# Decayed block attention and a SiLU layer on one core: the order of the up units, two state casts and two loads around chunks 8 to 11

## The chip, the core and the metric

The kernel runs on one core of a Trainium2 chip. The metric is device time in microseconds (us) of one execution; lower is better. Five engines work from queues of their own, each strictly in order, and wait for each other by semaphores: TensorE (PE in the profile; PEld is its loading of weights), VectorE (DVE), ScalarE (ACT), GpSimd (POOL) and SyncE (SP), which here only issues DMA transfers. ScalarE can issue transfers too; they then stand in its own queue between its other instructions.

## The reference: what is computed

Inputs are q, k, v of shape (4, 8, 768, 64) (batch, head, position, width), a decay `lam` per head, and two weight matrices. Per batch entry and head, in blocks of 64 positions:

```python
intra = np.einsum('bhic,bhjc->bhij', qb, kb) * Dmask[None]       # lam ** (i - j) for i >= j
intra = np.einsum('bhij,bhjd->bhid', intra, vb)
inter = np.einsum('bhid,bhde->bhie', qb * lam_pow[None], kv_state)
out[:, :, sl] = intra + inter
kv_state = lam_block * kv_state + np.einsum('bhsd,bhse->bhde', kb * rev_pow, vb)
...
h = x @ w_in                       # x: (3072, 512), heads side by side; w_in: (512, 2048)
g = h * (1.0 / (1.0 + np.exp(-h)))
return g @ w_out                   # w_out: (2048, 512)
```

(`lam_block` is written with its axes in the full text.) The output is 3072 x 512 float32.

## The kernel before

**Chunks and groups.** The 3072 tokens are 24 chunks of 128 (two attention blocks of 64 each; six chunks are one batch entry) and 12 groups of 256, so group g is made of chunks 2g and 2g+1. A chunk's attention comes first; its transposed output (`xt`) is the input of the dense layer of its group. The kernel's own schedule is kept as written: each engine's queue holds its instructions in the order in which the code emits them. Chunks 0 to 3 and groups 0 and 1 follow a list written out by hand (`ORDER`, L23). Everything that the change touches comes later and is written as loops from L902 on.

**What a chunk from 6 on goes through.** `load_qk` and `load_vs` (L880, L892) issue its q, k and v, 256 KB each, by `load_1` (L229), on SP unless an engine is named. The buffers: 4 for q (`qf`), 6 for k (`kf`), 6 for v (`vf`). `preps` (L897) scales q and k by the decay on GpSimd (L364, L365: two instructions each for q and k, four a chunk). `transposes` issues two DMA transposes on SP (L390, L391), which leave `qt` and `kn`. `vcast` (L382) rounds v to bfloat16 (`vb`), on ScalarE unless another engine is named. Then `section` (L438) does the attention with small 64 x 64 matmuls (L540), for up to three jobs at once: outputs (`op`) of the chunks `outs`, scores (`sp`) of the chunks `scores`, and state increments (`kv_ps`) of the half chunks `states`. Outputs need the masked scores (`ss`), `vb`, `qt` and the running states as bfloat16 (`kvs`). Behind the matmuls the section emits the move of the outputs to `xt`, the masking of the scores on VectorE (L560), and, for each half chunk of `states`, an addition to the running total on VectorE (`total`, L571 or L573) and a cast of it to `kvs` (L574, helper `move` at L176) on the engine named by `cast`. With `defer=True` this last part, additions and casts, is not emitted but handed back as a function, `finish`.

**What a group goes through.** Eight up units (`ups`, L951): unit i is 8 matmuls (`ffn1_mm`, L605) into one bank of 512 columns (`h_ps`, two such banks) and one SiLU on ScalarE (L621); it makes features 256 i to 256 i + 255. Units 2j and 2j+1 fill one tile `quad(g, j)`. The down product (`seven`, L731) does 7 half-width products where 8 would be plain, so it needs sums and differences of the SiLU's results as well: `gd` of one quad (`g_diff`, L711), and `gc` and `gb` of the quads j-2 and j (`g_cross`, L698), on VectorE. `ups` emits `g_diff` behind the units 1, 3 and 5 and `g_cross` behind 5 and 7; the last `gd` comes in the second product's step (`after_4`). The order of the products is 3, 4, 1, 6, 5, 2, 7: the first two take the SiLU's results directly, product 1 needs `gc`, 6 and 7 need `gd`, 5 and 2 need `gb`.

**The order around the change.** The lines from L922 on, in order: the scalings and transposes of chunks 4 and 5; pieces of the down product of groups 0 and 1 (`down0`); casts of the last weights; q and k of chunk 8, issued by ScalarE (L934); the section with scores of 4 and 5 and three states, cast by ScalarE (L936); three more pieces of down product; the scalings and transposes of 6 and 7; the section with the outputs of 4 and 5 (L941); two pieces of down product with `load_qk(9)` on SP between them (L943); the second half of the weight sums (L946). Then the loop over the groups 2 to 10 (L959), in which c and d are the chunks of the next group and a and b those of the one after it. In group 2 the scores of 6 and 7 come ahead of the third product and the outputs of 6 and 7 ahead of the sixth. In group 3 the scores of 8 and 9 come ahead of the last up unit (L971, `defer=True`); ahead of the third product stand the v casts of 10 and 11, then `late()` with the additions and casts for 8 and 9, then the scalings and transposes of 12 and 13 and more loads; ahead of the sixth product comes the section with outputs of 8 and 9, scores of 10 and 11 and their states (L993, states cast by GpSimd). From group 4 on each group has one section, ahead of its sixth product.

Of the kernel before, what the change touches and what calls it, by code (L numbers as in the profile page):

```python
# [36 lines left out]
def kernel(  # L37
# [10 lines left out]
    nc = tc.nc  # L48
# [121 lines left out]
    def cast_w(which, i, e="D", part=None):  # L170
        a, b = (0, 2) if part is None else (part, part + 1)
        ko, f = w_piece(which, i, a, b)
        t = wtmp[which, i]
        move(e, (w_in_bf if which == "in" else w_out_bf)[:, ko, f], t[part] if isinstance(t, list) else t[:, a:b, :])

    def move(e, dst, src):  # L176
        if e == "A":
            nc.scalar.activation(dst, src, AF.Copy)  # L178
        elif e == "P":
            nc.gpsimd.tensor_copy(dst, src)  # L180
        else:
            nc.vector.tensor_copy(dst, src)  # L182
# [46 lines left out]
    def load_1(src, c, tag, bufs, e=None):  # L229
        b, blk = divmod(c, NB)  # L230
        t = io.tile([128, H, D], F32, name=tag, tag=tag, bufs=bufs)
        (e or nc.sync).dma_start(out=t, in_=src[b, :, blk * BLK:(blk + 1) * BLK, :].rearrange("h s d -> s h d"))
        return t

    def load_k(c, e=None):
        rawk[c] = load_1(k, c, "kf", 6, e)
# [145 lines left out]
    def vcast(c, e="A"):  # L382
        if c in vraw:
            move(e, natb[c][2], vraw.pop(c).rearrange("s (p j) d -> s p j d", j=2))
# [40 lines left out]
    def new_xt(c):  # L425
        g, off = group_of[c]
        if off == 0:
            xt[g] = xpool.tile([128, KO_IN, GROUPS[g]], BF16, name="xt", tag="xt", padded_shape=[128, KO_IN, 512])
        return xt[g][:, :, off * BLK:(off + 1) * BLK]
# [8 lines left out]
    def section(outs=(), scores=(), states=(), e="AA", tags=(("att", 3),) * 2, spare=None, cast="D", defer=False):  # L438
# [33 lines left out]
        def place(c, h):  # L472
            w = [x for x, y in states if y == h].index(c)
            return kv[0][:, h] if shared else kv[h][:, w]
# [70 lines left out]
        for c in outs:  # L545
            x = new_xt(c)
        if outs:
            if len(outs) == 2:
                x = xt[group_of[outs[0]][0]]
            for i, op in enumerate(banks):  # L550
                if len(tags) == 4:
                    i, w = divmod(i, 2)
# [3 lines left out]
        if scores:  # L556
# [5 lines left out]
                both.append(ss)  # L562
            for w, c in enumerate(scores):
                st[c] = [ss[:, NP * w:NP * w + NP, :] for ss in both]
        def finish():
            for c, h in states:
                b = c // NB
                kvs = nat.tile([128, NP, D], BF16, name="kvs", tag="kvs", bufs=8)
                old, total[b] = total.get(b), nat.tile([128, NP, D], F32, name="total", tag="total", bufs=4)
                if old is None:  # L570
                    nc.vector.tensor_copy(total[b], place(c, h))  # L571
                else:
                    nc.vector.tensor_tensor(total[b], old, place(c, h), op=AL.add)  # L573
                move(cast, kvs, total[b])  # L574
                kvh[(c, 1) if h == 0 else (c + 1, 0)] = kvs

        if defer:
            return finish
        finish()

    kvh = {}
    mask64 = const.tile([128, 64], F32, name="mask64")
# [13 lines left out]
    total = {}  # L596
# [28 lines left out]
    def ffn1_two(g, i):  # L625
        tick()
        ffn1_open(g, i)
        ffn1_mm(g, i, range(KO_IN))
        ffn1_close(g, i)
# [68 lines left out]
    def g_cross(g, j):  # L698

        low, one = quad(g, j - 2), quad(g, j)  # L700
        cross = sum_tile(g, "gc", 0, 128)[:, j - 2]
        nc.vector.tensor_tensor(cross, low[:, :, lo], one[:, :, hi], op=AL.add)  # L702
        both = gpool.tile([128, 4, 256], BF16, name="gb", tag="g")
        nc.vector.tensor_tensor(both, low, one, op=AL.add)  # L704
        for u in range(4):
            k = 4 * (j - 2) + u
            gs[g, 1, k] = cross[:, u, :]
            gs[g, 5, k] = both[:, u, lo]
            gs[g, 2, k] = both[:, u, hi]

    def g_diff(g, j):  # L711

        one = quad(g, j)
        d = sum_tile(g, "gd", j // 2, 128)[:, j % 2]
        a, b = (hi, lo) if j < 2 else (lo, hi)
        nc.vector.tensor_tensor(d, one[:, :, a], one[:, :, b], op=AL.subtract)  # L716
        for u in range(4):
            gs[g, 6 if j < 2 else 7, 4 * (j % 2) + u] = d[:, u, :]
# [100 lines left out]
    for word in LOADS.split():  # L819
        a = int(word[2])  # L820
# [59 lines left out]
    def load_qk(*cs, e=None):  # L880
        for c in cs:
            if c < NCHUNK:
                rawq[c] = load_1(q, c, "qf", 4, e)
                load_k(c, e)
                loaded.append(c)

    def transposes(*cs):
        for c in cs:
            if c < NCHUNK:
                dma_t(c)  # L890

    def load_vs(*cs, e=None):  # L892
        for c in cs:
            if c < NCHUNK:
                load_v(c, e)

    def preps(*cs):  # L897
        for c in cs:
            if c < NCHUNK:
                prep(c)  # L900
# [16 lines left out]
    def down0(kk, *mts):  # L917
        for mt in mts:
            ffn2(mt // 2, mt % 2, range(4 * kk, 4 * kk + 4), tag="h" if mt > 1 else "o")
# [11 lines left out]
    copy_kt(5, tk5)  # L931
    vcast(4), vcast(5)
    cast_w("out", 6), cast_w("out", 7, "A", 0), cast_w("out", 7, "A", 1)
    load_qk(8, e=nc.scalar)  # L934
    down0(2, 0)
    section((), (4, 5), ((4, 0), (4, 1), (5, 0)), cast="A")  # L936
    down0(2, 1)
    down0(3, 2)
    down0(3, 3)
    preps(6, 7), transposes(6, 7)  # L940
    section((4, 5), (), (), "AD", (("att", 3), ("kv", 1), ("att", 3), ("att", 3)))  # L941
    down0(3, 0)
    load_qk(9)  # L943
    down0(3, 1)
    for i in range(len(WSUMS)):
        weight_sum(i, 1)  # L946
# [1 line left out]
    def steps(*cs):  # L948
        return [(c, h) for c, h in [(cs[0] - 1, 1)] + [(c, h) for c in cs for h in range(2)] if c > 5][:-1]

    def ups(g, i):  # L951
        ffn1_two(g, i)
        if i > 3 and i % 2:
            g_cross(g, i // 2)
        if i % 2 and i < 7:
            g_diff(g, i // 2)

    many = (("h", 2),) * 2 + (("att", 3),) * 2
    for g in range(2, len(GROUPS) - 1):  # L959
        c, d, a, b = range(2 * g + 2, 2 * g + 6)  # L960
        for i in range(8):
            if g == 2 and i == 4:
                preps(8, 9)
                load_qk(10)
                transposes(8, 9)
                load_vs(8, 9)
                load_qk(11)
            if g < 4 and i in (4, 5):
                vcast(c + i % 2)
            if g == 3 and i == 7:  # L970
                late = section((), (c, d), steps(c, d), cast="A", defer=True)  # L971
            ups(g, i)
        for i, unit in enumerate(seven(g)):
            if i == 2 and g > 2:
                vcast(a)
                if g == 3:
                    vcast(b)
                    late()
            if i == 2:
                preps(c + 4, d + 4)  # L980
                transposes(c + 4, d + 4)
                load_qk(*([12] if g == 2 else []), c + 7)
                load_vs(c + 6, d + 6)
                load_qk(d + 7)
            if i == 2 and g == 2:
                section((), (c, d), steps(c, d), cast="A")
            if i == 3 and g > 3:
                vcast(b)
            if i == 0 and g == 2:
                load_vs(10, 11)  # L990
            if i == 5:
                cs = [x for x in (a, b) if g > 2 and x < NCHUNK]
                section((c, d), cs, steps(*cs) if cs else (), "AD", many[:2] if cs else many, cast="P")  # L993
            unit()
    g = len(GROUPS) - 1
    for i in range(8):
        ups(g, i)
# [32 lines left out]
```

## Time and profile before

| what | us |
|---|---|
| median of 3 runs | 202.52 (200.32 to 202.88) |
| the profiled execution, its own time | 200.34 |
| its span, first to last instruction | 198.0 |
| TensorE busy with matmuls in the span | 188.5 |
| VectorE, ScalarE, GpSimd busy | 131.2, 102.3, 71.3 |
| group 2, from its first up matmul to that of group 3 | 47.90 to 63.49 |
| group 3 | 63.49 to 80.03 |
| group 4 | 80.03 to 94.94 |
| group 5 | 94.94 to 109.34 |

How to read it: the span is what the profile sees; 2.34 us of the execution's own time lie around it. The rows on groups are read off the chain of work that ended last, in order of time. A timeline line gives the start, the time taken, engine, line, operation, the names written and read, and the count; brackets give how long the engine stood idle before it and who ended that. ACTq and SPq are the queues of ScalarE and SP, with the issues of DMA transfers in them. Granted TensorE clock: 1.00 throughout.

### The profile page before, as it was taken

To read this page: it belongs to the slowest core of one execution; us is meant where nothing else is said; L and a number is where in the kernel's file an instruction comes from. 1 tells how busy PE (TensorE), PEld (TensorE's weight loads), DVE (VectorE), ACT (ScalarE), POOL (GpSimd) and SP (SyncE) were. 2 spreads that over 40 slices of the span, in tenths; PEclk is the share of its full clock that TensorE was granted. 3 is DMA by queue.
4 is the path that set the end of the run, shared out by engine and by line. 5 is a ranking of instruction groups with operands and counts; after the bars stand their busy time and mean duration, and the time that the engine had idled before them with its cause. 6 is when DMAs were issued, how large, how long until landed. Compare 5 with 4: busy or idle time off the path is not lost.

```text
span 198.0 us, 6663 instructions
## 1 busy us (share of the span) xinstructions
PE 188.5 (95%) x2844; PEld 151.1 (76%) x2844; DVE 131.2 (66%) x254; ACT 102.3 (52%) x192; POOL 71.3 (36%) x124
## 2 busy tenths in 40 slices
PE   7688999999999999999999999999999999999993
PEld 2457544546887887887888888888888887888882
DVE  1896459778986296985875855865785666565263
ACT  3874875153825855553554563563662752633621
POOL 5240000918826060793653724742760201200000
PEclk9999999999999999999999999999999999999999
DMA  3999999989679995995988949998999790200203
GB/s 105 338 370 404 403 408 304 243 235 271 115 171 129 208 192 131 204 203 125 213 121 202 196 111 227 144 207 221 126 310 368 111 358 22 106 0 3 109 0 106
DMA packets 95581, 38.71 MB, mean 196 GB/s; under 512 B 80960, under 2 KB 88640, under 8 KB 95552
## 3 DMA queue, kind: packets, MB, share of 16 engines
q1 hardware_dynamic: 93328, 37.76, 75.8%
q10 hardware_dynamic: 2224, 0.53, 1.2%
q8 instruction: 22, 0.36, 0.7%
q14 instruction: 7, 0.06, 0.1%
HBM read 27.27 MB, written 6.29 MB: 170 GB/s over the span
## 4 chain that ended last, share of the span: by engine, by line
PE 76%; DVE 7%; DMA 5%; POOL 3%; SPq 3%; ACT 3%; issue 2%; ACTq 0%; DVEq 0%; POOLq 0%
PE h_ps L609 32%; PE o_ps L729 23%; PE o_ps L654 6%; PE h_ps L843 5%; PE op L540 3%; SPq L224 2%; DMA pair<-in_q_dram 2%; PE o_last L729 2%; DVE ss L560 2%; PE sp L540 1%; DVE total L573 1%; DMA qf<-in_q_dram 1%; DMA kn<-kb 1%; ACT g L621 1%; POOL kvs L180 1%
## 5 line engine op out<-in xcount | busy, mean ns | idle before, releaser
L609 PE MATMUL h_ps<-xt,w_in_bf 128*128 128x256 bf16 x672 | 75.9, 273 | 0.0
L609 PEld LDWEIGHTS <-w_in_bf 128*128 128x128 bf16 x672 | 65.5, 98 | 8.5 <-issue 0.2
L621 ACT ACTIVATE g<-h_ps 128x512 bf16<-128x512 f32 x84 | 49.9, 597 | 33.5 <-PE h_ps L609 33.5
L364 POOL TENSOR_TENSOR qb<-qf,lam_fwd 128x256 bf16<-128x256 f32 x18 | 12.0, 667 | 40.5 <-issue 25.4
L716 DVE TENSOR_TENSOR gd<-g 128x512 bf16<-128x512 bf16 x40 | 20.5, 515 | 8.2 <-ACT g L621 8.0
L180 POOL CAST kvs<-total 128x256 bf16<-128x256 f32 x26 | 11.0, 433 | 25.6 <-DVE total L573 20.0
L178 ACT ACTIVATE xt<-op 128x256 bf16<-128x256 f32 (+1 forms) x18 | 8.3, 486 | 21.9 <-PE op L540 20.9
L729 PE MATMUL o_ps<-w_out_bf,gb 128*128 128x256 bf16 x144 | 18.9, 273 | 0.5 <-issue 0.5
L182 DVE CAST xt<-op 128x256 bf16<-128x256 f32 (+1 forms) x16 | 8.3, 543 | 16.1 <-PE op L540 14.4
L729 PE MATMUL o_ps<-wsum,gd 128*128 128x256 bf16 x144 | 18.7, 273 | 0.0
L702 DVE TENSOR_TENSOR gc<-g 128x512 bf16<-128x512 bf16 x20 | 9.7, 484 | 13.2 <-ACT g L621 13.2
L729 PE MATMUL o_ps<-wsum,g 128*128 128x256 bf16 x144 | 17.2, 273 | 0.0
L729 PEld LDWEIGHTS <-g 128*128 128x128 bf16 x160 | 15.7, 98 | 1.8
L729 PEld LDWEIGHTS <-gd 128*128 128x128 bf16 x160 | 15.6, 98 | 1.8
L729 PEld LDWEIGHTS <-gb 128*128 128x128 bf16 x160 | 14.9, 98 | 2.6 <-issue 0.6
L364 POOL TENSOR_TENSOR kb<-kf,lam_bwd 128x256 bf16<-128x256 f32 x20 | 14.6, 731 | 3.9 <-DMA kf<-in_k_dram 2.9
L704 DVE TENSOR_TENSOR gb<-g 128x1024 bf16<-128x1024 bf16 x20 | 15.9, 798 | 0.0
L573 DVE TENSOR_TENSOR total<-total,kv_ps 128x256 f32<-128x256 f32 x33 | 13.8, 419 | 2.2
L654 PE MATMUL o_ps<-w_out_bf,g 128*128 128x512 bf16 x64 | 15.0, 379 | 0.1
L365 POOL TENSOR_TENSOR kb<-kf,lam_bwd 128x256 bf16<-128x256 f32 x20 | 14.4, 718 | 0.0
L365 POOL TENSOR_TENSOR qb<-qf,lam_fwd 128x256 bf16<-128x256 f32 x18 | 13.0, 721 | 0.0
L560 DVE TENSOR_TENSOR ss<-sp,mask 128x512 bf16<-128x512 f32 x20 | 12.8, 681 | 0.0
(105 smaller groups left out, 247.0 us busy)
## 6 DMA issues: line engine op xcount, KB each, us to landing
vf<-in_v_dram SPq DMA_DIRECT2D x20, 256.0 KB, 4.4
kf<-in_k_dram SPq DMA_DIRECT2D x19, 256.0 KB, 4.7
qf<-in_q_dram SPq DMA_DIRECT2D x17, 256.0 KB, 4.2
pair<-in_moe_w_out_dram SPq DMA_DIRECT2D x8, 512.0 KB, 7.7
pair<-in_moe_w_in_dram SPq DMA_DIRECT2D x6, 512.0 KB, 7.5
out_dram<-pair SPq DMA_DIRECT2D x12, 256.0 KB, 3.8
out_dram<-ob SPq DMA_DIRECT2D x10, 256.0 KB, 3.8
pair<-in_k_dram SPq DMA_DIRECT2D x4, 256.0 KB, 4.5
```

Of the source, the lines that this page charges most:

```text
L180: nc.gpsimd.tensor_copy(dst, src)
L364: eng.tensor_tensor(dst[:, 0::2], src[:, 0::2, ::-1, :], by[:, 0::2, ::-1, :], op=AL.mult)
L365: eng.tensor_tensor(dst[:, 1::2], src[:, 1::2], by[:, 1::2], op=AL.mult)
L560: nc.vector.tensor_tensor(ss, sp.rearrange("k w p q -> k (w p) q"), mask64[:, None, :].to_broadcast([128, len(scores) * NP, D]), op=AL.mult)
L573: nc.vector.tensor_tensor(total[b], old, place(c, h), op=AL.add)
L609: nc.tensor.matmul(hps[g, i][:, a:a + 256], lhsT=w_in_bf[:, ko, m * 128:(m + 1) * 128], rhs=xt[g][:, ko, :], start=(ko == 0 and u == 0), s ...
L621: nc.scalar.activation(gg.rearrange("p u n -> p (u n)"), hps[g, i], AF.Silu)
L654: nc.tensor.matmul(o, lhsT=gt[g, ko][:, mt * BLK:(mt + 1) * BLK], rhs=w_out_bf[:, ko, :], start=(ko == 0), stop=(ko == KO_OUT - 1))
L704: nc.vector.tensor_tensor(both, low, one, op=AL.add)
L716: nc.vector.tensor_tensor(d, one[:, :, a], one[:, :, b], op=AL.subtract)
L729: nc.tensor.matmul(dst, lhsT=lhsT, rhs=rhs, start=(start and k == 0), stop=(k == K2 - 1), skip_group_check=True)
L843: nc.tensor.matmul(hps["m", m], lhsT=w_in_bf[:, ko, m * 128:(m + 1) * 128], rhs=xall[0][:, :, ko, :], start=(ko == 0), stop=(ko == KO_IN - 1))
```

## The change

Five edits, one text:

- q and k of chunk 9 are issued by ScalarE directly behind those of chunk 8; the issue on SP at L943 goes.
- `ups` takes a position n and does the units in the order 0, 1, 4, 5, 2, 3, 6, 7, in all groups from 2 on. What follows a unit (`g_diff`, `g_cross`) goes with it.
- In group 3 the section with scores and states of chunks 8 and 9 is emitted ahead of the seventh position in place of the eighth.
- A deferred section now hands back a function that emits the additions alone and gives the list of casts. In group 3 the additions are emitted behind the unit of the seventh position, and the four casts, still on ScalarE, ahead of the third product.
- The v casts of 10 and 11 in group 3 go from ScalarE to GpSimd, where they stand ahead of the scalings of 12 and 13.

```diff
--- before.py
+++ after.py
@@ -562,7 +562,8 @@
                 both.append(ss)
             for w, c in enumerate(scores):
                 st[c] = [ss[:, NP * w:NP * w + NP, :] for ss in both]
-        def finish():
+        def sums():
+            casts = []
             for c, h in states:
                 b = c // NB
                 kvs = nat.tile([128, NP, D], BF16, name="kvs", tag="kvs", bufs=8)
@@ -571,12 +572,15 @@
                     nc.vector.tensor_copy(total[b], place(c, h))
                 else:
                     nc.vector.tensor_tensor(total[b], old, place(c, h), op=AL.add)
-                move(cast, kvs, total[b])
+                casts.append((kvs, total[b]))
+                if not defer:
+                    move(cast, *casts[-1])
                 kvh[(c, 1) if h == 0 else (c + 1, 0)] = kvs
+            return casts
 
         if defer:
-            return finish
-        finish()
+            return sums
+        sums()
 
     kvh = {}
     mask64 = const.tile([128, 64], F32, name="mask64")
@@ -931,7 +935,7 @@
     copy_kt(5, tk5)
     vcast(4), vcast(5)
     cast_w("out", 6), cast_w("out", 7, "A", 0), cast_w("out", 7, "A", 1)
-    load_qk(8, e=nc.scalar)
+    load_qk(8, 9, e=nc.scalar)
     down0(2, 0)
     section((), (4, 5), ((4, 0), (4, 1), (5, 0)), cast="A")
     down0(2, 1)
@@ -940,7 +944,6 @@
     preps(6, 7), transposes(6, 7)
     section((4, 5), (), (), "AD", (("att", 3), ("kv", 1), ("att", 3), ("att", 3)))
     down0(3, 0)
-    load_qk(9)
     down0(3, 1)
     for i in range(len(WSUMS)):
         weight_sum(i, 1)
@@ -948,7 +951,9 @@
     def steps(*cs):
         return [(c, h) for c, h in [(cs[0] - 1, 1)] + [(c, h) for c in cs for h in range(2)] if c > 5][:-1]
 
-    def ups(g, i):
+    def ups(g, n):
+
+        i = (0, 1, 4, 5, 2, 3, 6, 7)[n]
         ffn1_two(g, i)
         if i > 3 and i % 2:
             g_cross(g, i // 2)
@@ -967,16 +972,20 @@
                 load_qk(11)
             if g < 4 and i in (4, 5):
                 vcast(c + i % 2)
-            if g == 3 and i == 7:
-                late = section((), (c, d), steps(c, d), cast="A", defer=True)
+            if g == 3 and i == 6:
+                sums = section((), (c, d), steps(c, d), defer=True)
             ups(g, i)
+            if g == 3 and i == 6:
+                late = sums()
         for i, unit in enumerate(seven(g)):
-            if i == 2 and g > 2:
+            if i == 2 and g > 3:
                 vcast(a)
+            if i == 2 and g == 3:
+                for x in late:
+                    move("A", *x)
+            if i == 2:
                 if g == 3:
-                    vcast(b)
-                    late()
-            if i == 2:
+                    vcast(a, "P"), vcast(b, "P")
                 preps(c + 4, d + 4)
                 transposes(c + 4, d + 4)
                 load_qk(*([12] if g == 2 else []), c + 7)
```

## The prediction

> **What bounds the kernel now.** I read the page first, then the busy time by window, then TensorE's timeline wherever a window shows less than a full PE, then what those gaps waited for.
>
> ```profile
> PE 188.5 (95%) x2844; PEld 151.1 (76%) x2844; DVE 131.2 (66%) x254; ACT 102.3 (52%) x192; POOL 71.3 (36%) x124
> ...
> q10 hardware_dynamic: 2224, 0.53, 1.2%
> ```
>
> TensorE is the bound: 188.5 of 198.0 us. The first 20 us and the last 4 hold most of the 9.5 us without a matmul, and the change touches neither. From 20 us on, only a stall of PE is worth time. The second line is ScalarE's DMA queue: today it carries two loads of 256 KB (q and k of chunk 8) and little else. The change gives it four.
>
> ```profile
> 75.80:78.10 2.30, 1.90 (x129) 1.54 (x128) 0.92 (x3) 0.99 (x3) 0.00 (x0) 1.00 0.39 89
> 91.30:93.00 1.70, 1.33 (x121) 1.17 (x120) 0.00 (x0) 0.00 (x0) 0.00 (x0) 1.00 0.44 99
> 106.30:107.50 1.20, 1.20 (x122) 1.16 (x122) 0.00 (x0) 0.00 (x0) 0.30 (x1) 1.00 1.21 272
> ```
>
> Each window is one attention section (outputs of two chunks, scores and states of the next two) inside a group. The columns are the window, its length, then busy time and count of PE, PEld, DVE, ACT, POOL. The section of some 128 small matmuls takes 1.2 us when nothing is late (106.3; the next ones, read off the chain, take 1.23, 1.21, 1.13). It takes 2.3 at 75.8 and 1.7 at 91.3: 1.1 and 0.5 us lost.
>
> ```profile
> 61.03 0.22 PE L540 MATMUL op<-qt,kvs 64*64 64x64 bf16 x4 [0.23 <-ACT kvs L178]
> ...
> 76.47 0.22 PE L540 MATMUL op<-qt,kvs 64*64 64x64 bf16 x2 [0.17 <-ACT kvs L178]
> ...
> 76.92 0.22 PE L540 MATMUL op<-qt,kvs 64*64 64x64 bf16 x2 [0.23 <-ACT kvs L178]
> ...
> 92.27 0.32 PE L540 MATMUL sp<-qt,kn 64*64 64x64 bf16 x16 [0.37 <-DMA kn<-kb]
> ```
>
> The brackets say who was late: at 61.0 and 76.5 a state cast on ScalarE, at 92.3 a transposed k. VectorE's and SP's timelines say why:
>
> ```profile
> 73.98 0.41 DVE L763 TENSOR_TENSOR msum<-msum,o_ps 128x256 f32<-128x256 f32 x1
> 74.31 0.41 DVE L716 TENSOR_TENSOR gd<-g 128x512 bf16<-128x512 bf16 x1
> 74.64 1.77 DVE L573 TENSOR_TENSOR total<-total,kv_ps 128x256 f32<-128x256 f32 x4
> ```
>
> The four totals of chunks 8 and 9 end at 76.4, behind a VectorE that has had no break since 69.7. Their matmuls were done at 70.4.
>
> ```profile
> 76.21 0.57 SPq L232 DMA_DIRECT2D qf<-in_q_dram  x1
> 76.84 0.57 SPq L232 DMA_DIRECT2D kf<-in_k_dram  x1
> 77.45 0.83 SPq L232 DMA_DIRECT2D qf<-in_q_dram  x1
> 78.33 2.12 SPq L232 DMA_DIRECT2D kf<-in_k_dram  x1
> ```
>
> This is a burst of four 256 KB loads on one queue. The first two issues cost 0.57 us each, the third 0.83, the fourth 2.12. In the trace's packet records a load is 1040 packets; counting those issued and not yet started, an issue that would carry its queue past about 2,600 ends only when the count is down to 2,650 (third load here), or as low as 1,392 (the fourth). Other bursts: the fourth issue took 0.80 at 93.4, 0.80 at 106.2, 0.83 at 143.8. The issuing engine stands still meanwhile.
>
> ```profile
> 42.84 0.41 ACTq L232 DMA_DIRECT2D qf<-in_q_dram  x1
> 43.34 0.54 ACTq L232 DMA_DIRECT2D kf<-in_k_dram  x1
> 43.36 0.61 ACT L178 ACTIVATE w_out_bf<-pair 128x512 bf16<-128x512 f32 x1
> 43.92 1.14 ACT L178 ACTIVATE kvs<-total 128x256 bf16<-128x256 f32 x3
> ```
>
> ScalarE's queue in order: two issues, and 0.04 us behind the second the state casts (L178) that the output section of chunks 4 and 5 needs. They end at 45.06; PE enters that section at 45.2. So there is 0.2 us of room where the change puts two more issues.
>
> **The change part by part.** All durations are of the profiled execution: span 198.0, own time 200.34, so 2.34 lie around the span. The median of the runs shown is 202.52 (200.32 to 202.88): the profile stands at the low end.
>
> *q and k of chunk 9 on ScalarE.* SP loses two issues (53.86 and 54.53, 1.1 us). ScalarE gains them at 43.9, in front of the three state casts. Loads three and four of a burst meet the queue's limit. By 45.15 the 2080 packets of today's two loads had dropped by 480, and by 47.1 by 1520: with the limit near 2,640 the third issue ends at 45.15 and the fourth at 47.1. The casts then run 47.15 to 48.3 instead of 43.92 to 45.06. PE has nothing else: its queue is in order, and only this section and, behind it, two pieces of down product (1.83 us) stand before group 2. Half a section (32 matmuls) after a late cast took 0.61 us at 61.0, so it ends at 48.9 instead of 46.07: **+2.8**. Lower bound: both issues cost a bare 0.57 and 0.53, the casts end at 46.25, **+0.8**. Upper bound: the fourth issue ends like the one at 78.33, with 1,392 or less left, that is after some 2,900 packets; at the 590 per us of 44.5 to 47.9 that is 49.4, so **+5.1**. I take 2.8, since the limit near 2,640 fits third issues everywhere and more than half of the fourth ones, and the queue it meets here drains no faster than SP's. The casts of x behind the section (0.76 us) are still hidden by the 1.83.
>
> The Trainium skill speaks to this too. Its page "DMA: Bandwidth & Descriptors", section "Issuing engines are not separate DMA queues", says that issuing from a second engine saves only the sequencer's time for issuing, usually small against the transfer. Taken at its word this prices the move at two short issues, the lower bound; the row at 78.33, with 2.12 us for one issue, speaks against "small" in a burst.
>
> The four loads also share the engines with v of 6 and 7 and the transposes of 6 and 7 on SP, by up to 2080 packets, 2 us. k of 7 is issued for transposing at 52.59 and takes 2.4 to land, 55.0; scores of 6 and 7 ran at 56.8 and come at 59.6 with the stall above: cover 2.6. Without the stall the cover would be 1.8 and a few tenths could be lost.
>
> *SP's queue after it.* SP issues nearly without a break from 53.86 to 92. Two issues fewer there shift the rest by 1.1 us at least, and q, k of 10 no longer queue behind them (55.11 took 1.77). Transposed k of 13 was 0.4 late at 92.3; it is now 1.1 earlier while PE is later: **-0.5** (0 to -0.5). K of 11 landed at about 77.3 (74.95 + 2.4), which also held the section at 75.8; it gets the same relief.
>
> *Totals of chunks 8 and 9 earlier.* The section's scores and states move one unit (0.88 us) ahead, and the totals stand in VectorE's queue in front of the last gc and gb instead of behind the last gd. By VectorE's rows: gc, gb, gd of unit 5 run after the fourth unit's silu (67.6) to 69.5, gd to 70.1, masks to 71.3, totals to 73.1, then gc at 73.4, where it ended in the run before. ScalarE casts the four states (4 x 0.42) after msum at 73.6, so they are ready at 75.3, before PE needs them at 75.8. The v casts of 10 and 11 that stood there (1.14 us) are GpSimd's. So the excess goes: **-1.1** (-0.4 if only the bracketed idle goes). The products ahead of it took 4.55 instead of 4.37; **-0.1** of that.
> What is late next: the section comes at 68.6 and its last 16 state matmuls at 69.05, while v of 9 is cast by 69.2: **+0.15** (0 to 0.4).
>
> *v of 10 and 11 on GpSimd.* No row has it; a 256-wide cast took 0.43 and a 512-wide scaling 1.1, so 0.9 to 1.1 each, some 2 us. GpSimd stood idle from 73.0 to 79.55, waiting for q of 12. Nothing. If that load comes early, the preparation of 12 and 13 is up to 2 us later, against some 4 us between its ends (85.5) and the need of PE.
>
> *Up units in another order, in all groups.* Same matmuls, same silus; gc and gb move two units ahead. From 94.8 on groups take 14.4 us and their sections do not wait, so nothing to win; buffers of the pool come free in the earlier group's products. 0.
>
> Sum: 198.0 + 2.8 + 0.15 - 1.1 - 0.5 - 0.1 = 199.25, own time 201.6, that is +1.25 or 0.6%. From the median it would be 203.8. As the known times of before lie half at 200.3 and half at 202.5 to 202.9, I state the middle, **202.6**.
>
> **The rivals.**
> *Issues stay short* (the page's rule): +0.8 in place of 2.8, so -0.75, 199.6 from the profile, 201.8 from the median. For it: today's two issues took 0.41 and 0.54 while SP's own were held up. Against: third and fourth in every SP burst.
> *The fourth issue ends late*: +5.1, sum +3.55: 203.9 from the profile, 206.1 from the median. It is slower by over 2% once ScalarE is held past some 49.9 (+4.05). For it: 2.12 at 78.33, 2.40 at 94.21. Against: 0.8 in other bursts.
> *The section at 75.8 stays slow*, since GpSimd's casts or k of 11 come last in place of the totals: 1.6 of gains lost, +2.95: 203.3 and 205.5.
> *Faster by over 2%* needs 4 us; all stalls after 20 us that the change reaches are 1.8. Nothing in the change reaches the rest.
>
> **How the numbers follow.** Forecast 0.52, short issues 0.22, late fourth issue 0.13, section stays slow 0.10, something else 0.03. The range runs from 199.6 (short issues, from the profile) to 205.6 (section slow, from the median); it leaves out most of the late issue from the median. A measurement here tells about 2% from no change, 4 us. Faster by that: 0.03. Slower: half of the late issue and a little of the rest, 0.08. Within: 0.89.
>
> **What would show it.** After: four issues on ScalarE from 42.8, the last ending near 47; state casts near 47.2; PE idle for 2 to 3 us before op at 48; section at about 78.5 and 94 in 1.2 us each; totals ahead of the second gc. Wrong if the state casts start before 45.3, or if a section after 75 still waits for kvs, vb or kn.

## The result, and the profile after

Over 20 runs of each the changed kernel has a median of 202.84 us (201.49 to 204.6), the kernel before 201.4 (199.43 to 202.88). The ratio is 1.0091, 95% interval 1.0066 to 1.0116: slower by 0.9%, some 1.8 us; the two medians lie 1.44 apart. The ratio leaves out executions in a slower state, two of the changed kernel's 20. The profiled execution has a span of 201.0 us against 198.0.

The page of the kernel after, PE's busy time and ScalarE's DMA queue:

```profile
PE 192.3 (96%) x2844; PEld 154.2 (77%) x2844; DVE 133.3 (66%) x254; ACT 101.0 (50%) x190; POOL 71.7 (36%) x126
...
q10 hardware_dynamic: 4304, 1.05, 2.4%
```

ScalarE's queue now carries twice the bytes. What that does stands in ScalarE's timeline of the kernel after:

```profile
43.66 0.40 ACTq L232 DMA_DIRECT2D qf<-in_q_dram  x1
44.16 0.54 ACTq L232 DMA_DIRECT2D kf<-in_k_dram  x1
44.19 0.61 ACT L178 ACTIVATE w_out_bf<-pair 128x512 bf16<-128x512 f32 x1
44.73 2.00 ACTq L232 DMA_DIRECT2D qf<-in_q_dram  x1
46.82 1.57 ACTq L232 DMA_DIRECT2D kf<-in_k_dram  x1
48.74 1.03 ACT L178 ACTIVATE kvs<-total 128x256 bf16<-128x256 f32 x3 [3.94 <-issue]
```

The third and fourth issue take 2.00 and 1.57 us, and the three state casts start 4.58 us after the second issue began, where it was 0.58. TensorE's timeline of the kernel after, its waits between 40 and 96 us:

```profile
49.22 0.22 PE L540 MATMUL op<-qt,kvs 64*64 64x64 bf16 x4 [2.22 <-ACT kvs L178]
...
65.19 0.22 PE L540 MATMUL op<-qt,kvs 64*64 64x64 bf16 x4 [0.17 <-ACT kvs L178]
...
65.65 0.22 PE L540 MATMUL op<-qt,kvs 64*64 64x64 bf16 x4 [0.23 <-ACT kvs L178]
```

The new wait is the 2.22 us; the one of the section of group 2 is still there, with 0.17 us more ahead of it; those at 76 and 92 are gone. The two sections by window (window, length, then busy time and count of PE, PEld and so on):

```profile
80.30:81.60 1.30, 1.30 (x130) 1.26 (x130) 0.00 (x0) 0.00 (x0) 1.30 (x4) 1.00 1.02 232
94.80:96.00 1.20, 1.20 (x122) 1.16 (x122) 0.00 (x0) 0.00 (x0) 1.20 (x4) 1.00 1.12 254
```

They took 2.3 and 1.7. VectorE's timeline of the kernel after shows why the first is on time:

```profile
75.83 1.78 DVE L574 TENSOR_TENSOR total<-total,kv_ps 128x256 f32<-128x256 f32 x4
77.52 0.42 DVE L706 TENSOR_TENSOR gc<-g 128x512 bf16<-128x512 bf16 x1
```

The totals end at 77.6, 2.7 us before the section; before, they ended 0.6 us after its start.

To compare profiles I use stretches of TensorE's order of work, counted from its first score matmul of chunks 4 and 5 (in the traces: 41.59 before, 43.40 after):

| stretch | before | after | difference | predicted |
|---|---|---|---|---|
| start to the scores of 4 and 5 | 41.59 | 43.40 | +1.81 | 0 |
| those scores to group 2 | 6.15 | 8.71 | +2.56 | +2.8 |
| group 2 | 15.59 | 15.84 | +0.25 | 0 |
| group 3 | 16.54 | 15.32 | -1.22 | -1.05 |
| group 4 | 14.91 | 14.44 | -0.47 | -0.5 |
| group 5 to the end | 103.2 | 103.3 | +0.1 | 0 |

The first row is not the change's: the code up to there is the same. The sixteen score matmuls of the first attention chunks (L288) took 0.64 us each time in this profile and 0.42 in that of before; sixteen output matmuls (L323) took 0.64 us at 15.75 and 0.42 at 17.57. The trace's records of a full granted clock begin at 17.25 us here and at 4.43 in the profile of before, so this row goes with a slower clock at the start. The profiles of the later runs have this stretch at 41.57 to 43.12; in three that issue loads of chunk 9 on ScalarE too it is 41.57. Without the first row the profiles differ by 1.2 us.

### The profile page after: what moved, and what is told of

It reads as the page before. It is cut to its first block, busy times and chain, and to the rows that moved or that the text cites. A ratio compares the mean times of both kernels' runs of the same rounds, so it can differ in the third digit from the quotient of the medians.

```text
span 201.0 us, 6672 instructions
## 1 busy us (share of the span) xinstructions
PE 192.3 (96%) x2844; PEld 154.2 (77%) x2844; DVE 133.3 (66%) x254; ACT 101.0 (50%) x190; POOL 71.7 (36%) x126
## 3 DMA queue, kind: packets, MB, share of 16 engines
q10 hardware_dynamic: 4304, 1.05, 2.4%
## 4 chain that ended last, share of the span: by engine, by line
PE 84%; DVE 8%; DMA 2%; ACTq 2%; ACT 1%; issue 1%; SPq 0%; DVEq 0%
PE h_ps L613 33%; PE o_ps L733 26%; PE o_ps L658 6%; PE h_ps L847 5%; PE op L540 3%; DMA pair<-in_q_dram 2%; DVE wsum L689 2%; PE o_last L733 2%; ACTq L232 2%; PE sp L540 2%; PE sp L288 1%; PE tq L269 1%; DVE gd L720 1%; DVE ss L560 1%; PE kv_ps L540 1%; PE op L323 1%
## 5 line engine op out<-in xcount | busy, mean ns | idle before, releaser
L180 POOL CAST kvs<-total 128x256 bf16<-128x256 f32 x26 | 10.2, 401 | 38.7 <-DVE total L574 28.3
L364 POOL TENSOR_TENSOR qb<-qf,lam_fwd 128x256 bf16<-128x256 f32 x18 | 12.6, 698 | 29.7 <-DMA qf<-in_q_dram 21.8
L706 DVE TENSOR_TENSOR gc<-g 128x512 bf16<-128x512 bf16 x20 | 11.0, 548 | 13.3 <-ACT g L625 13.3
L708 DVE TENSOR_TENSOR gb<-g 128x1024 bf16<-128x1024 bf16 x20 | 17.0, 849 | 0.0
L540 PE MATMUL op<-qt,kvs 64*64 64x64 bf16 x296 | 10.1, 195 | 2.7 <-ACT kvs L178 2.6
```

The costliest lines, as they stand in the source:

```text
L364: eng.tensor_tensor(dst[:, 0::2], src[:, 0::2, ::-1, :], by[:, 0::2, ::-1, :], op=AL.mult)
L540: ins = nc.tensor.matmul(dst, lhsT=lhsT, rhs=rhs, start=start, stop=True, skip_group_check=True)
```

## The experiments

Every kernel ran beside the kernel before on one chip. Theory: ScalarE stands still at its third and fourth load because its queue of transfers is full, and the state casts behind them are late. Rival A: issues are short, and other edits lose. Rival B: the transfers themselves are in the way.

**Loads of chunk 9 back on SP, the rest of the change kept.**

```diff
-    load_qk(8, 9, e=nc.scalar)
+    load_qk(8, e=nc.scalar)
...
     down0(3, 0)
+    load_qk(9)
     down0(3, 1)
```

> The whole change, but q and k of chunk 9 issued by SP again, between the two last pieces of down product. Theory (ScalarE stands at its third and fourth load, because its queue of transfers is full, and the state casts of chunks 4 and 5 behind them are late): from the first score matmul of chunks 4 and 5 to group 2 takes 6.2 us again (8.8 with the change), the section of group 3 keeps its gain, the one of group 4 may be late again by up to 0.5; in all 1.2 to 1.7 us under the kernel before, ratio 0.992 to 0.994. Rival A (an issue costs half a us, and the other edits are what loses): no faster than before, ratio 1.00 or more. Rival B (the engines of the transfers are too busy between 43 and 50): as the theory, this run does not tell it apart.

Measured: ratio 0.9935 (0.9899 to 0.9971), so this is faster than both kernels. 5.86 us to group 2; groups 2, 3 and 4 take 15.59, 15.96 and 14.44. Its wait in group 3, in TensorE's timeline of this run:

```profile
76.45 0.22 PE L540 MATMUL sp<-qt,kn 64*64 64x64 bf16 x2 [0.35 <-DMA kn<-kb]
```

As the theory has it; rival A is out. What is left of group 3 (15.96 against 15.32) is for the most part the wait for the transposed k of 11 (`kn`), with SP's two issues back in its queue. Group 4 takes 14.44 as in the changed kernel, although SP issues these loads again.

**The kernel before with the loads moved and nothing else.**

```diff
-    load_qk(8, e=nc.scalar)
+    load_qk(8, 9, e=nc.scalar)
...
-    load_qk(9)
```

> The kernel before with one edit: q and k of chunk 9 issued by ScalarE behind those of chunk 8. Theory: 8.8 us from the scores of 4 and 5 to group 2, that is 2.6 lost; the section of group 3 keeps the late totals (some 0.4 to 1.1 lost as before), the one of group 4 is on time (0.5 won); ratio 1.010 to 1.013. Rival A: 0.8 lost and 0.5 won, ratio 1.00 to 1.002. Rival B: as the theory.

Measured: ratio 1.0138 (1.0081 to 1.0195), 8.45 us to group 2, issues three and four 2.24 and 1.52 us, group 4 at 14.52. As the theory; the ratio is a little over the 1.013 given. Group 2 took 16.19 instead of 15.59, with the units in their old order: so it is the loads and not the new order that lengthen it.

**The loads on ScalarE, behind the outputs of chunks 4 and 5.**

```diff
-    load_qk(8, 9, e=nc.scalar)
+    load_qk(8, e=nc.scalar)
...
+    load_qk(9, e=nc.scalar)
     down0(3, 0)
     down0(3, 1)
```

> The whole change, but ScalarE issues q and k of chunk 9 behind the section with the outputs of chunks 4 and 5 (three instructions further in its queue: state casts and the cast of x come first). Theory: the state casts run at 44 to 45 as before and nothing is late; the issues end before ScalarE's first SiLU of group 2; 6.2 to 6.4 us to group 2, sections of groups 3 and 4 in 1.2 us; 1.6 us under the kernel before, ratio 0.990 to 0.993. Rival A: ratio as the whole change less 0.8, about 1.005. Rival B (the transfers themselves are in the way of those of 6 and 7): the loss stays for the most part, since they still run between 46 and 52; ratio over 1.002.

Measured: ratio 0.9999 (0.9971 to 1.0027). The state casts are on time (5.86 us to group 2), as expected, but group 2 takes 16.73 and group 3 15.85. ScalarE's timeline of this run:

```profile
46.76 0.37 ACTq L232 DMA_DIRECT2D qf<-in_q_dram  x1
47.03 0.38 ACT L178 ACTIVATE xt<-op 128x256 bf16<-128x256 f32 x1
50.17 0.37 ACTq L232 DMA_DIRECT2D kf<-in_k_dram  x1
50.59 1.08 ACT L625 ACTIVATE g<-h_ps 128x512 bf16<-128x512 f32 x2 [3.18 <-PE h_ps L613]
```

The issues are short here, 0.37 us each, but between them lie 3 us. In the trace's records the second one waits until 50.12 for a semaphore (number 102) on which the load of k of chunk 8 counts; that load's last packets end at 49.4. The transfers share eight such semaphores in turn, and the new one was given that one. The first SiLU of group 2 stands behind it, and TensorE waits 0.83 us at 51.2. This wait was in none of the theories. It is the larger part of what group 2 lost (16.73 against 15.59 with the loads on SP); in group 3 TensorE waits 0.36 us for `gc`. The ratio under 1.002 speaks against rival B, though its interval reaches 1.0027.

**State casts of 4 and 5 on VectorE, four loads on ScalarE.**

```diff
-    section((), (4, 5), ((4, 0), (4, 1), (5, 0)), cast="A")
+    section((), (4, 5), ((4, 0), (4, 1), (5, 0)), cast="D")
```

> The whole change, but the three state casts of chunks 4 and 5 are made by VectorE behind its additions; ScalarE still issues four loads in a row. Theory: the casts no longer wait for the issues and end near 45.6; the section of 4 and 5 loses 0.5 at most; but ScalarE's half of the cast of x stands behind the fourth issue (to about 48.4 on the clock of before) and holds group 2 by about 1.2; 7.2 to 7.7 us to group 2 instead of 8.8; ratio 0.998 to 1.004. Rival A and B: what the casts wait for is not ScalarE's queue, so about 8.8 us and the ratio of the whole change, 1.009.

Measured: ratio 1.0041 (1.0011 to 1.0070), 6.37 us to group 2, less than expected: the last two issues took 1.57 and 1.96 us and ended at 46.6, in time for ScalarE's half of the cast of x. With another engine for the casts 2.3 of the 2.6 us are gone though all four loads are issued as before: what held the section was ScalarE's queue. The ratio lies just over the 1.004 given, while the profiled execution, the shortest of this run's, has a span 0.3 under that of before; the reading rests on the profile. Group 3 took 16.26, since the product with `gc` came 0.77 us too early for VectorE:

```profile
74.63 0.61 PE L733 MATMUL o_ps<-wsum,gc 128*128 128x256 bf16 x4 [0.77 <-DVE gc L706]
```

**Three loads on ScalarE: q of 9 there, k of 9 on SP.**

```diff
-    load_qk(8, 9, e=nc.scalar)
+    load_qk(8, e=nc.scalar)
+    rawq[9] = load_1(q, 9, "qf", 4, nc.scalar)
...
     down0(3, 0)
+    load_k(9)
     down0(3, 1)
```

> The whole change, but of the two loads moved only q of chunk 9 is issued by ScalarE; k of chunk 9 is issued by SP between the two last pieces of down product. Theory (a full queue holds the issue): the third issue on ScalarE still takes 1.5 to 2 us, not half a us, and the state casts of 4 and 5 start some 1.5 us after those of the run with both loads on SP; from the scores of 4 and 5 to group 2 takes 7.0 to 7.6 us, between 5.9 (both on SP) and 8.7 (both on ScalarE). Ratio 0.997 to 1.003. Rival A (short issues): 0.4 to 0.5 lost at most, 6.3 us or less, ratio 0.995.

Measured: ratio 0.9979 (0.9932 to 1.0026), 7.19 us to group 2. The issues, in ScalarE's timeline of this run:

```profile
42.73 0.41 ACTq L232 DMA_DIRECT2D qf<-in_q_dram  x1
43.23 0.54 ACTq L232 DMA_DIRECT2D kf<-in_k_dram  x1
43.80 1.55 ACTq L232 DMA_DIRECT2D qf<-in_q_dram  x1
45.40 1.03 ACT L178 ACTIVATE kvs<-total 128x256 bf16<-128x256 f32 x3 [1.53 <-DVE pair L664]
```

Here the third issue is the last one and is long, and each of the two costs about half of the loss (5.86, 7.19, 8.71). In group 3 (16.17) TensorE waits 0.68 us for `gc`.

**The same bytes in half as many packets.** The four loads on ScalarE read rows of 512 bytes.

```diff
+        if e is nc.scalar:
+            e.dma_start(out=t.rearrange("p (h r) d -> p h (r d)", r=2),
+                        in_=src[b, 0:4, blk * BLK:(blk + 2) * BLK, :].rearrange("h (p r) d -> p h (r d)", r=2))
+            return t
```

> The whole change, but the four loads that ScalarE issues read rows of 512 bytes (four heads of two rows) in place of 256: the same 256 KB each in half as many packets, 528. It reads other positions for q and k of chunks 8 and 9, so those values are not the reference's; all times are comparable. Theory (the queue holds an issue by the number of its packets not yet started, limit about 2,600): four loads are 2,112, so all four issues take 0.4 to 0.7 us, the state casts start 2 to 3 us earlier than with the change, 6.0 to 6.8 us to group 2 in place of 8.7; ratio 0.992 to 0.999. Rival (bytes not yet moved, or a busy memory): the third and fourth issue still take 1.5 to 2 us each, 8 us or more to group 2, ratio 1.005 or more.

Measured: ratio 0.9998 (0.9966 to 1.0031), 7.13 us to group 2. ScalarE's timeline of this run:

```profile
42.82 0.41 ACTq L233 DMA_DIRECT2D qf<-in_q_dram  x1
43.32 0.46 ACTq L233 DMA_DIRECT2D kf<-in_k_dram  x1
43.82 0.60 ACTq L233 DMA_DIRECT2D qf<-in_q_dram  x1
44.52 0.46 ACTq L233 DMA_DIRECT2D kf<-in_k_dram  x1
45.34 1.03 ACT L178 ACTIVATE kvs<-total 128x256 bf16<-128x256 f32 x3 [1.37 <-DVE pair L668]
```

All four issues are short with the same bytes. The queue holds an issue by packets, not by bytes. Two other causes are out by the records: the completion semaphores that the third and fourth issue of the changed kernel use had been complete since 43.63 and 45.47, before these issues began; and SP issues v of two chunks beside ScalarE's issues in both kernels (3.02 us after, 2.66 here), so SP's issuing does not hold ScalarE's. The 7.13 is above the 6.0 to 6.8 expected: two short issues cost 1.3 us against the loads on SP, since besides 0.6 and 0.46 some 0.4 us pass between the last issue and the first cast. So of the loss of 2.85 against that run (8.71 less 5.86) 1.3 is for two issues at all and 1.6 for the full queue. The ratio is just over the 0.992 to 0.999 expected: group 4 takes 15.24 and waits 0.68 us for `kn`, although SP has two issues fewer here too.

**The units in their old order**, loads on SP, rest of the change.

```diff
-        i = (0, 1, 4, 5, 2, 3, 6, 7)[n]
+        i = n
```

> Loads of chunk 9 on SP, the rest of the change, but the up units in the order 0 to 7 in all groups. Theory (the order matters in group 3 alone, where VectorE has the earlier totals in front of the last gc): unit 5 then comes sixth, its gc, gb and gd stand directly before the masks and totals, the last gc ends some 1.5 us later than with the new order, and product 1 of group 3 waits for it; group 3 takes 0.5 to 1.5 us longer than with the new order (16.5 to 17.4 in place of 15.96), groups from 4 on are the same within 0.1. Ratio 0.997 to 1.003. Rival: the order is worth nothing, ratio 0.9935, group 3 at 16.0.

Measured: ratio 0.9974 (0.9937 to 1.0012); group 3 takes 16.87 in place of 15.96, all later groups are the same within 0.06. TensorE's timeline of this run:

```profile
74.86 0.61 PE L733 MATMUL o_ps<-wsum,gc 128*128 128x256 bf16 x4 [1.18 <-DVE gc L706]
```

In the old order the earlier totals make `gc` 1.2 us late; the new order takes this wait away. It does not always do so: in five of the other runs with the new order `gc` of group 3 is still 0.34 to 0.77 us late. In the profile the rival is out; the timed ratio alone does not separate it from 0.9935.

**v of 10 and 11 back on ScalarE**, loads on SP, rest of the change.

```diff
-                    vcast(a, "P"), vcast(b, "P")
+                    vcast(a), vcast(b)
```

> Loads of chunk 9 on SP, the rest of the change, but v of chunks 10 and 11 cast by ScalarE behind the four state casts. Theory: the state casts end near 75.3 on the clock of before, the v casts 1.1 later, so the state matmuls of the section of group 3 wait 0.3 to 0.6 us; but transposed k of 11, which held that section with the loads on SP, lands at about the same time, so little is added: group 3 16.0 to 16.4, ratio 0.993 to 0.997. Rival: GpSimd's casts slow VectorE and cost as much as they give; group 3 shorter than 15.96, ratio under 0.993.

Measured: ratio 0.9990 (0.9949 to 1.0031). Group 3 takes 16.13, its wait is 0.66 us for `kn` and none for `vb`; group 4 takes 14.88 and waits 0.32 for `kn`. The ratio is over the 0.997 expected, though its interval reaches down into the range. With no wait for `vb`, the run does not show that GpSimd's casts are worth anything; whether the later `kn` of groups 3 and 4 belongs to this edit stays open.

**The loads on ScalarE between SiLUs of group 2.**

```diff
-    load_qk(8, 9, e=nc.scalar)
+    load_qk(8, e=nc.scalar)
...
+            if g == 2 and i == 2:
+                rawq[9] = load_1(q, 9, "qf", 4, nc.scalar)
+            if g == 2 and i == 3:
+                load_k(9, nc.scalar)
```

> The whole change, but ScalarE issues q of chunk 9 ahead of the third SiLU of group 2 and k ahead of the fourth. Theory: its queue of transfers is empty by then, so each issue takes 0.4 to 0.6 us and lies under the SiLU before it; the state casts of 4 and 5 are on time (6.0 to 6.2 us to group 2), SP keeps its two issues fewer, so k of 11 is in time for the section of group 3 (15.3 to 15.6); ratio 0.988 to 0.992, better than with the loads on SP. Rival B (the transfers, not the issues, are in the way): no better than 0.9935, and group 2 longer than 15.9.

Measured: ratio 0.9982 (0.9944 to 1.0021), not better than with the loads on SP. The issues took 0.38 and 0.45 us, no SiLU was late, and 5.86 us to group 2: all as expected. But group 2 took 16.08, which is the sign that was given for rival B, and group 3 15.84, with 0.34 us of waiting for `gc`; group 4 took 14.76. VectorE's timeline of this run, in group 2:

```profile
53.23 0.83 DVE L720 TENSOR_TENSOR gd<-g 128x512 bf16<-128x512 bf16 x1
53.98 0.83 DVE L706 TENSOR_TENSOR gc<-g 128x512 bf16<-128x512 bf16 x1
...
55.34 1.59 DVE L720 TENSOR_TENSOR gd<-g 128x512 bf16<-128x512 bf16 x2
```

and of GpSimd:

```profile
52.92 0.86 POOL L364 TENSOR_TENSOR qb<-qf,lam_fwd 128x256 bf16<-128x256 f32 x1 [0.77 <-DMA qf<-in_q_dram]
53.74 0.79 POOL L365 TENSOR_TENSOR qb<-qf,lam_fwd 128x256 bf16<-128x256 f32 x1
```

Each `gd` and `gc` takes 0.83 us where it took 0.41 beside an idle GpSimd. Earlier loads make GpSimd prepare chunk 9 earlier, and that now lies beside VectorE's chain. The next run tests this alone.

**Four more scalings on GpSimd**, loads on SP, rest of the change; their results are not read.

```diff
-                preps(8, 9)
+                raw8 = rawq[8].rearrange("s (p j) d -> s p j d", j=2)
+                preps(8)
+                for _ in range(2):
+                    spare = nat.tile([128, NP, 2, D], BF16, name="spare", tag="spare", bufs=1)
+                    crosswise(nc.gpsimd, spare, raw8, decay(lam_fwd, 2))
+                preps(9)
```

> The kernel with the loads of chunk 9 on SP and the rest of the change, with four more scalings on GpSimd (256 wide, into a tile that nobody reads) between the preparations of chunks 8 and 9, where GpSimd stands idle for 4.3 us; they wait for nothing new. Theory (what earlier loads cost in group 2 is GpSimd's work running beside VectorE's weight sums, gd, gc and gb, which take up to twice as long then): group 2 takes 15.9 to 16.3 us in place of 15.59, VectorE's gb and gd there 1.0 and 0.75 in place of 0.6 and 0.33; ratio 0.995 to 0.999. Rival (it is the transfers, which are unchanged here): group 2 15.6, ratio 0.9935.

Measured: ratio 1.0105 (1.0037 to 1.0173). VectorE's timeline of this run, and TensorE's waits in the section of group 2:

```profile
53.53 0.83 DVE L720 TENSOR_TENSOR gd<-g 128x512 bf16<-128x512 bf16 x1
54.29 0.83 DVE L706 TENSOR_TENSOR gc<-g 128x512 bf16<-128x512 bf16 x1
55.04 1.10 DVE L708 TENSOR_TENSOR gb<-g 128x1024 bf16<-128x1024 bf16 x1
```

```profile
60.49 0.26 PE L540 MATMUL op<-ss,vb 64*64 64x64 bf16 x8 [0.33 <-DVE ss L560]
61.27 0.22 PE L540 MATMUL op<-qt,kvs 64*64 64x64 bf16 x4 [0.53 <-ACT kvs L178]
61.72 0.22 PE L540 MATMUL op<-qt,kvs 64*64 64x64 bf16 x4 [0.17 <-ACT kvs L178]
62.18 0.22 PE L540 MATMUL op<-qt,kvs 64*64 64x64 bf16 x4 [0.23 <-ACT kvs L178]
```

Those waits are 1.26 us; the run with the loads on SP has 0.23 there. So GpSimd's work beside VectorE is enough to lengthen group 2, as the theory says, with the transfers unchanged; that the transfers add nothing in the run between SiLUs is not shown. Group 2 took 18.14, far more than expected, and the ratio missed its range: 1.0 of the 2.55 us over 15.59 is the longer waits, the other 1.5 goes with a fall of the clock, told at the end. Without it the 16.6 is still over the 15.9 to 16.3 expected.

## Why the prediction came out

The direction held, and so did the place and the size of the main loss: +0.6% was forecast, +0.9% came, and 202.84 stands beside 202.6. Part of that closeness is luck: two terms have other causes than the working gave, a loss in group 2 was missed, and the gap between profiles and timed runs is not explained.

*The loads on ScalarE*: forecast +2.8, measured +2.56 to group 2 against the kernel before, and 2.85 against the run that keeps all else and has the loads on SP. The mechanism was right: third and fourth issue long, state casts behind them, TensorE with nothing else to do. The two issues took 2.00 and 1.57, 3.6 together where 3.2 was forecast from the queue's drain; packets counted as in the prediction, they ended with some 2,170 and 2,290 not yet started, below the 2,640 taken as the limit. The run with half the packets shows that packets are what counts, and the run with the casts on VectorE that ScalarE's queue is what the section waited for.

*The lower bound of that term* was mis-sized: two short issues were priced at +0.8 from their bare length and cost 1.3 in the run with short issues. The rival of short issues failed: they were 2.00 and 1.57 us, and on this engine even short ones lie on the path. The Trainium skill, "DMA: Bandwidth & Descriptors", section "Issuing engines are not separate DMA queues", calls the sequencer's time for issuing usually small against the transfer; this case's trace does not agree for these two, with 3.2 to 7.3 us from issue to landing for the loads of that stretch.

*SP's queue*: forecast -0.5 in group 4, measured -0.47. The number is met, but the runs do not tie it to the two issues: with the loads back on SP group 4 takes 14.44 as well (14.88 in the run with v on ScalarE), and with the loads on ScalarE it took 15.24 in the run with half the packets. What appears with the loads on SP is the wait for k of 11 in group 3, 0.35 and 0.66 us in two of those runs.

*The earlier totals*: forecast -1.1 -0.1 +0.15, measured -1.22 in group 3; the section of scores ran 0.1 us longer than before, within the 0 to 0.4 given. Not all of it is the totals': with the loads on SP the same edits give -0.58 (16.54 to 15.96), and the other 0.64 comes only with the loads moved, for the most part as k of 11 in time. The prediction named that relief and gave it no term of its own.

*The units' order, priced at 0*, holds from group 4 on. In group 3 it is a part of the other term: without it group 3 takes 0.9 us longer, by `gc`. The working of that term used the new order, so the sum was right and its attribution was not.

*v on GpSimd, priced at nothing*: the two casts took 1.36 us together, not 2, in time that GpSimd had free. Beside them, though, one `gb` of VectorE took 1.09 us, 0.68 in the run with v on ScalarE; the prediction had no word on that.

*What was missed* is +0.25 in group 2 (+0.6 in the run with the loads alone): q and k of 9 land earlier and those of 10 are issued earlier, so GpSimd prepares both chunks earlier. In the profile after, chunk 9's scalings lie beside VectorE's weight sums and chunk 10's (58.1 to 61.5) beside its `gd`, `gc` and `gb`, which then take up to twice as long. The prediction looked at what GpSimd's order holds up and not at whom it slows.

Three figures in the working do not come out: 4,160 packets less 1,392 are 2,768 and not some 2,900, which makes the upper bound about +4.9; 1.25 and 1.6 of lost gains make +2.85 and not +2.95; and the load at 94.21 is the fifth of its burst, not the fourth. None of them enters the forecast's sum; the second one reaches the upper end of the range, by 0.1.

The profile-based sum of +1.25 meets 1.2 in the profiles, without the start. The timed ratio is 1.8 us, and what makes up the rest stays open. Among runs with a mean granted clock of 1.00 the medians are 202.02 (7 runs) and 200.84 (29 runs of before beside the experiments), 1.2 apart. The changed kernel's 13 runs under that have a median of 203.42; but the 48 such runs of before have 200.98, hardly more than the others, so a lower clock alone does not explain it. A late start of the full clock, as in the profile after, is a candidate that no run tests.

## What to carry to other kernels

A load that an engine issues between its own instructions costs that engine its issue, and the cost is not constant: count what the queue still holds, in packets, before pricing it at half a microsecond. Put issues where nothing that is waited for stands behind them, and look at the completion semaphore the new transfer shares. When a load comes earlier, ask which engine then works earlier and whom it slows down; and an addition put ahead on a full engine has to be paid for by work moved behind it. Test each term by a run of its own: here two terms met their numbers, and the runs did not bear out the whole of the cause given.

## What the runs showed of the hardware that was not expected

The granted clock fell to one half for 3.41 us, from 63.07, in the run with more GpSimd work, right behind the section in which TensorE had been busy for 1.54 of 2.80 us. By window (the last three columns are clock, DMA share, GB/s):

```profile
60.00:62.80 2.80, 1.54 (x59) 1.03 (x58) 1.94 (x5) 1.47 (x4) 2.80 (x6) 1.00 1.10 198
62.80:66.40 3.60, 3.60 (x19) 2.63 (x20) 1.78 (x4) 1.04 (x3) 0.35 (x1) 0.54 0.54 64
66.40:70.00 3.60, 3.60 (x35) 3.18 (x33) 0.78 (x2) 1.95 (x4) 0.00 (x0) 0.99 1.08 244
```

It goes with about 1.5 of the 18.14 us of that group. Four of the twelve profiles, this one among them, have one more such fall of 3.41 us, at 11 to 12.5 us. In the profiled execution of the changed kernel the stall of 2.22 us had no such effect: TensorE was busy for 1.38 of 3.70 us from 46.7 and the clock stayed at 1.00. What decides it was not tried. Over the timed runs the mean granted clock is 0.991 for the changed kernel and 0.996 for the kernel before.

An instruction of VectorE with two inputs took up to twice as long beside GpSimd's scalings (0.41 to 0.83 for 512 wide, 0.68 to 1.10 for 1024), and GpSimd's scalings 0.62 to 1.06 beside VectorE's.
